# Loading two tokens to a partition in 512-byte rows for the first four units of a retention and FF kernel

## The chip, the cores and the metric

The kernel runs on one core of a Trainium2 chip. The metric is device time in microseconds (us) of one execution. Most executions of one kernel lie within about 1% of their mean here; each comparison with the kernel before was made on the same chip in the same rounds. The experiments ran in four sets with their own rounds and chips, so between sets the ratios say more than the medians. Every ratio is the mean time of one kernel's fast runs over the mean of the other's fast runs of the same rounds, so it is not quite the ratio of the medians that stand beside it.

## The reference, cut to what matters

```python
# q, k, v: (8 batches, 8 heads, 576 tokens, 64), fp32
scores = q @ k.T / 8
ret    = scores * Dmat                  # Dmat[i, j] = gamma_h ** (i - j) for i >= j, else 0
attn   = ret @ v
x      = attn, heads joined: (4608, 512)
out    = relu(x @ w_in) ** 2 @ w_out    # w_in (512, 2048), w_out (2048, 512)
```

The retention part is computed by chunks of 128 tokens ("units", 36 of them, 32 full and 4 made of tails of 64) with a state R that is carried from one chunk to the next. The FF part is most of the arithmetic.

## The kernel before: the parts that the change touches

Every instruction is a task in a small model of the machine inside the program. The model has durations and priorities (keys), and the order in which it starts the tasks is the order in which they are emitted. Each engine then has its own list in that order. An entry that waits can hold up those behind it: in run e11 below TensorE stands still for 2.53 us at one such entry, with FF work behind it.

```python
FIRST = ["u0", "u1", "u2", "u3", "w0", "w1", ..., "w7"]      # four units, then 8 weight blocks of 1 MB
WARM = 48                                                    # filler matmuls for the empty start

def add_load(u):                                             # on SyncE, three loads of 256 KB
    nc.sync.dma_start(out=x, in_=src[b, :, c*P:(c+1)*P, :].rearrange("h p d -> p h d"))   # rows of 64*4 = 256 B

def add_unit(u, base):
    # kq16 <- cast of k (GpSimd) and of q (ScalarE for the first four units, else GpSimd)
    # v16  <- v * vdec (GpSimd)
    # units 0..7: 8 transposes on TensorE into psT, then ScalarE (k) and VectorE (q) copy psT to kqT
    # units 8..:  one transposing DMA on SyncE writes kqT

# then, for each group of one or two units:
#   psc (scores), psS (chunk sums)      TensorE
#   rT = psc * mask, Rm, stmp, R        VectorE   (R is the state that the next unit reads)
#   psO (output)                        TensorE
#   xT = psO * gamma                    VectorE   -> the input of the FF
#   ph = xT @ w_in ; rl = relu ; gT = rl*rl ; po = gT @ w_out
# from group 3 on po is done by Strassen's scheme, which needs differences of weights, wT (VectorE)
```

Units 0 and 1 are groups of their own; units 2 and 3 are the third group, 4 and 5 the fourth. The SyncE queue holds loads, transposing DMAs and stores of the output in one list.

## Time and profile before

| | before |
|---|---|
| median, 6 runs (lowest to highest) | 303.44 us (302.53 to 305.68) |
| span of the profiled run | 301.3 us |
| TensorE busy | 286.8 us, 95% |
| DMA, 256 B rows / 2 KB rows | 219 / 383 GB/s |
| first FF matmul | 22.55 us |
| cast of the last weight block begins | 40.48 us |

How such a profile is read. An engine's busy share is an average over stages; what a stage is worth is read from what ended the wait there. A line of a timeline gives start and duration in us, engine, source line, operation, output<-inputs, and in brackets the idle time before it with what ended it. A line of the waits gives an engine's instruction, what released it, the total in us, the number of times and the longest. The prediction below shows the main lines of before. One thing it touches only in a figure is the hole at 134 us, so here is TensorE's timeline around its end, and the windows view of five microseconds of it (length, busy, count, granted clock, DMA share, GB/s):

```profile
133.38 0.60 PE L640 MATMUL ph<-xT,w_in 128*128 128x256 f16 x4
...
137.81 0.32 PE L307 MATMUL psc<-kqT 64*64 64x64 f16 x16 [3.46 <-DMA kqT<-kq]
138.06 1.47 PE L733 MATMUL po<-w_out,gS 128*128 128x256 f16 x8
139.33 1.92 PE L733 MATMUL po<-wT,gT 128*128 128x256 f16 x8
```

```profile
135.00:136.00 1.00, 0.00 (x0) 1.00 0.02 2
136.00:137.00 1.00, 0.00 (x0) 1.00 0.63 133
...
139.00:140.00 1.00, 1.00 (x7) 0.50 1.35 217
140.00:141.00 1.00, 1.00 (x6) 0.50 1.35 218
141.00:142.00 1.00, 1.00 (x6) 0.52 1.36 221
```

TensorE stands still for 3.46 us until a transposing DMA brings kqT, and then the granted clock is 0.50 for some 3.4 us. Half of 3.4 us is lost too, so the hole costs 3.46 + 1.7 = 5.2 us. From 135 to 136 us the DMA moved only 2 GB/s, so TensorE waits here for one chain and not for bytes in general: a q load issued at 127.86 us, its cast, and the transposing DMA issued at 132.90 (the 12th of the kernel, for unit 19). "Supply" below means such chains.

One profile shows one such slow stretch, which makes a mean clock of about 0.994 (an estimate: 1.7 of 301 us lost). Of the 104 runs of the kernel before in the experiments' rounds, 103 have a mean clock of 0.983 to 0.994, and 53 of them 0.989 or less. So nearly every run has at least one slow stretch, and about half seem to have a second, which the kept profile of before does not show.

### The profile page before, as it was taken

Reading aid. Unit: us, or ns where it says so; the run is one execution under the profiler, and the core shown is the slowest. Engines: PE = TensorE matmul, PEld = TensorE weight load, DVE = VectorE, ACT = ScalarE, POOL = GpSimd, SP = SyncE. Lnnn points to the kernel's source line nnn. Section 1 sums busy time; section 2 is a strip of 40 time slices with the busy share of each in tenths; the row PEclk is TensorE's granted clock in tenths of the full one; section 3 lists DMA queues with packets and bytes.
Section 4 is the critical chain, followed back from the end, with each engine's and each line's share of the span. In section 5 each row is a group of like instructions: output and inputs, shape, how many; then the busy total and the mean of one; then the engine's idle time right before and its main releaser. Section 6 shows DMA issues by size and latency. Waiting matters only on the chain.

```text
span 301.3 us, 10320 instructions
## 1 busy us (share of the span) xinstructions
PE 286.8 (95%) x4456; PEld 235.7 (78%) x4456; DVE 189.6 (63%) x409; ACT 186.6 (62%) x351; POOL 94.9 (31%) x125
## 2 busy tenths in 40 slices
PE   5988999999999999987999999999999999999995
PEld 2547865588888888865888888888888888888874
DVE  1476589777693949582876778567777676562410
ACT  4235972296757676741758575857585758558861
POOL 3433379434432332343242433243353200000000
PEclk9999999999999999997999999999999999999999
DMA  8999999889999997999999999999999520101012
GB/s 165 218 349 383 386 228 247 175 198 162 210 212 179 202 183 182 184 234 186 198 196 225 180 211 179 195 189 232 214 204 196 128 72 2 72 3 70 2 70 72
DMA packets 151742, 54.16 MB, mean 180 GB/s; under 512 B 142864, under 2 KB 143120, under 8 KB 151696
## 3 DMA queue, kind: packets, MB, share of 16 engines
q1 hardware_dynamic: 151248, 52.97, 90.2%
q8 instruction: 35, 0.57, 0.9%
q10 hardware_dynamic: 448, 0.52, 0.7%
q14 instruction: 11, 0.09, 0.1%
HBM read 36.70 MB, written 9.44 MB: 153 GB/s over the span
## 4 chain that ended last, share of the span: by engine, by line
PE 82%; DMA 6%; SPq 4%; DVE 3%; ACT 2%; issue 2%; POOL 1%
PE ph L640 41%; PE po L733 30%; PE psO L307 4%; SPq L263 4%; PE po L681 4%; DMA wi<-in_moe_w_in_dram 3%; DVE wT L597 2%; DMA kqT<-kq 2%; PE psc L307 2%; PE psS L307 2%; DMA q<-in_q_dram 1%; ACT rl L648 1%; ACT gT L658 1%; DVE xT L530 0%; POOL w_in L288 0%
## 5 line engine op out<-in xcount | busy, mean ns | idle before, releaser
L640 PE MATMUL ph<-xT,w_in 128*128 128x256 f16 (+1 forms) x1216 | 139.2, 268 | 1.7 <-POOL w_in L288 1.2
L640 PEld LDWEIGHTS <-w_in 128*128 128x128 f16 x1216 | 112.4, 98 | 15.5 <-POOL w_in L288 1.3
L648 ACT ACTIVATE rl<-ph 128x512 f16<-128x512 f32 x144 | 84.4, 588 | 49.8 <-PE ph L640 48.3
L658 ACT ACTIVATE gT<-rl 128x512 f16<-128x512 f16 x112 | 70.5, 630 | 3.5
L711 DVE TENSOR_TENSOR gS<-gT 128x512 f16<-128x512 f16 x60 | 29.9, 498 | 39.0 <-ACT gT L658 38.3
L333 POOL TENSOR_TENSOR v<-v,vdec_full 128x512 f16<-128x512 f32 x32 | 34.6, 1082 | 53.7 <-DMA v<-in_v_dram 49.6
L733 PEld LDWEIGHTS <-gS 128*128 128x128 f16 x480 | 46.0, 98 | 6.2 <-DVE gS L711 0.5
L733 PE MATMUL po<-wT,gS 128*128 128x256 f16 x360 | 49.0, 273 | 0.0
L733 PEld LDWEIGHTS <-gT 128*128 128x128 f16 x360 | 35.4, 99 | 4.5
L321 POOL CAST kq<-q 128x512 f16<-128x512 f32 x32 | 21.5, 673 | 39.1 <-DMA q<-in_q_dram 39.1
L321 POOL CAST kq<-k 128x512 f16<-128x512 f32 x36 | 23.7, 658 | 31.4 <-DMA k<-in_k_dram 28.3
L733 PE MATMUL po<-w_out,gT 128*128 128x256 f16 x240 | 31.1, 273 | 0.0
L530 DVE TENSOR_TENSOR xT<-psO,gam_full 128x512 f16<-128x512 f32 x36 | 23.9, 685 | 9.3 <-PE psO L307 9.0
L469 DVE TENSOR_TENSOR rT<-psc,mask 128x512 f16<-128x512 f32 x36 | 24.2, 685 | 8.7 <-PE psc L307 7.7
L660 DVE TENSOR_TENSOR gT<-rl 128x512 f16<-128x512 f16 x32 | 17.2, 549 | 12.3 <-ACT rl L648 12.1
L681 PE MATMUL po<-w_out,gT 128*128 128x512 f16 (+1 forms) x112 | 22.7, 349 | 0.3 <-ACT w_out L288 0.3
L756 DVE TENSOR_TENSOR o<-po,u 128x256 f32<-128x256 f32 x30 | 12.6, 419 | 11.0 <-ACT u L746 7.0
L227 PE MATMUL warm<-junk,ident 128*128 128x512 f16 x48 | 15.0, 451 | 3.0 <-DVE junk L205 3.0
L746 ACT COPY u<-po 128x256 f32<-128x256 f32 x30 | 11.0, 365 | 10.7 <-PE po L733 10.7
L498 DVE TENSOR_TENSOR R<-stmp,dec 128x256 f16<-128x256 f32 x32 | 16.4, 511 | 1.1
L681 PEld LDWEIGHTS <-gT 128*128 128x128 f16 x112 | 10.7, 98 | 8.0 <-issue 0.6
L776 ACT COPY o<-po 128x256 f32<-128x256 f32 x15 | 5.5, 367 | 18.2 <-PE po L733 18.1
(57 smaller groups left out, 253.0 us busy)
## 6 DMA issues: line engine op xcount, KB each, us to landing
k<-in_k_dram SPq DMA_DIRECT2D x32, 256.0 KB, 4.8
q<-in_q_dram SPq DMA_DIRECT2D x32, 256.0 KB, 4.7
v<-in_v_dram SPq DMA_DIRECT2D x32, 256.0 KB, 5.0
out_dram<-o SPq DMA_DIRECT2D x31, 256.0 KB, 3.2
wi<-in_moe_w_in_dram SPq DMA_DIRECT2D x4, 1024.0 KB, 10.4
wo<-in_moe_w_out_dram SPq DMA_DIRECT2D x4, 1024.0 KB, 9.2
k<-in_k_dram SPq DMA_DIRECT2D x8, 128.0 KB, 4.2
q<-in_q_dram SPq DMA_DIRECT2D x8, 128.0 KB, 4.7
```

Of the source, the lines that this page charges most:

```text
L307: nc.tensor.matmul(out_, lhsT=lhsT, rhs=rhs, start=start, stop=True, skip_group_check=True, tile_position=(64 * row, 64 * col))
L321: op(out=out_.rearrange("p (n b a d) -> p n b a d", n=2, b=2, a=2), in_=in_.rearrange("p (n a b) d -> p n b a d", n=2, a=2))
L333: nc.gpsimd.tensor_tensor(out=t, in0=tile_of["v32", u], in1=vdec[kind].rearrange("p (h o) -> p h o", o=1).to_broadcast([P, H, D]), op=ALU. ...
L469: nc.vector.tensor_tensor(out=r, in0=tile_of["psc", g][:, :, cols(s)].rearrange("p a (n i) -> p a n i", i=64), in1=mask.rearrange("p (o r ...
L530: nc.vector.tensor_tensor(out=tile_of["x", g][:, :, s * P:(s + 1) * P].rearrange("p n (c i) -> p c n i", c=2), in0=tile_of["psO", g][:, :, ...
L640: nc.tensor.matmul(tile_of["ph", g, fb][:, j, :], lhsT=w_in16[:, m, fi * P:(fi + 1) * P], rhs=tile_of["x", g][:, m, :], start=(m == 0), st ...
L648: nc.scalar.activation(out=t, in_=tile_of["ph", g, fb], func=ACTF.Relu)
L658: nc.scalar.activation(out=t, in_=rl, func=ACTF.Square)
L660: nc.vector.tensor_tensor(out=t, in0=rl, in1=rl, op=ALU.mult)
L681: nc.tensor.matmul(tile_of["po", u, lo], lhsT=tile_of["g", g][:, fi, s * P:(s + 1) * P], rhs=w_out16[:, fi, lo:hi], start=(fi == 0), stop= ...
L711: nc.vector.tensor_tensor(out=Sx(k, h), in0=in0(h), in1=in1(h), op=op)
L733: nc.tensor.matmul(tile_of["pb", g, bank], lhsT=left(i), rhs=right[:, i, :], start=(start and i == 0), stop=(i == HF - 1), skip_group_chec ...
```

## The change

Its intent: bring the first four units in faster, as their rows of 256 B move at 219 GB/s and the weights' at 383. Two neighbouring tokens of one head are contiguous in memory, so a partition that takes two tokens gets rows of 512 B. For k transposed and q transposed that layout does no harm (the copy from PSUM puts the tokens back in order), but k and v are also used with one token in a partition; matmuls with two 0/1 matrices bring them there. The pairs use the weights' buffers, the order of loads becomes pair, two weight blocks, pair, six blocks, and the R multiplications of these units go to GpSimd. Cut to its core:

```diff
+    perm = const.tile([P, 2, 2, P], FP16, name="perm")
+    nc.gpsimd.memset(perm, 0.0)
+    for s in range(2):
+        nc.gpsimd.affine_select(out=perm[:, s], ..., fill=1.0, base=-P * s, pattern=[[1, 2], [-1, P]], channel_multiplier=2)
-    WARM = 48
+    WARM = 40
+    PAIRED = 4
-    FIRST = ["u0", "u1", "u2", "u3", "w0", "w1", "w2", "w3", "w4", "w5", "w6", "w7"]
+    FIRST = ["p0", "w0", "w1", "p2", "w2", "w3", "w4", "w5", "w6", "w7"]
+    def add_load_pair(u):
+        for n, (name, src) in enumerate((("k", k), ("q", q), ("v", v))):
+            ... stage.tile([P, 2, H, 2 * D], FP32, name="pair", tag="wst")
+            nc.sync.dma_start(out=x, in_=src[b, :, c * P:(c + 2) * P, :].rearrange("h (p e) d -> p h (e d)", e=2))
+            loaded[...] = dma_task(0, 1.4 if loaded else 2.3, fn, ...)
+    def add_unit_pair(u, base):
+        # casts kx (GpSimd), qx (ScalarE), vx (GpSimd): 128x1024
+        # psT: 8 transposes each of kx and qx; copies to kqT reorder the tokens
+        for s in range(2):
+            for i, name in enumerate("kv"):
+                for e in range(2):
+                    nc.tensor.matmul(t, lhsT=perm[:, s, e, :], rhs=tile_of[name + "x", u][:, e, :], start=(e == 0), stop=(e == 1))
+                # k: ScalarE copies psn to kn;  v: VectorE multiplies psn by vdec into v16
-                nc.vector.tensor_tensor(          # R
+                (nc.gpsimd if u < PAIRED else nc.vector).tensor_tensor(
... (buffers are freed later accordingly)
```

More of the change, by code (lines that the diff above doesn't have):

```diff
@@ L161 @@
     make_identity(nc, ident)
+    perm = const.tile([P, 2, 2, P], FP16, name="perm")
+    nc.gpsimd.memset(perm, 0.0)
+    for s in range(2):
+        nc.gpsimd.affine_select(out=perm[:, s], in_=perm[:, s], compare_op=ALU.not_equal, fill=1.0, base=-P * s,
+                                pattern=[[1, 2], [-1, P]], channel_multiplier=2)
     iota_p = const.tile([P, 1], FP32, name="iota_p")
@@ L268, in add_load, with fn @@
             loaded[name, u] = dma_task(0, 1.2 if loaded else 2.1, fn, acq=("ld",) if n == 0 else ())
+    def add_load_pair(u):
+        b, c = units[u][1:]
+        for n, (name, src) in enumerate((("k", k), ("q", q), ("v", v))):
+            def fn(n=n, name=name, src=src):
+                if name != "q":
+                    tile_of["stage", u] = stage.tile([P, 2, H, 2 * D], FP32, name="pair", tag="wst")
+                x = tile_of[name + "32", u] = tile_of["stage", u][:, n % 2]
+                nc.sync.dma_start(out=x, in_=src[b, :, c * P:(c + 2) * P, :].rearrange("h (p e) d -> p h (e d)", e=2))
+            loaded[name, u] = loaded[name, u + 1] = dma_task(0, 1.4 if loaded else 2.3, fn,
+                                                             acq=("wst",) if name != "q" else ())
     def add_weight(i):
@@ L292, in add_weight @@
         wcast[i] = halves
-    ahead = 4
     for x in FIRST:
-        (add_load if x[0] == "u" else add_weight)(int(x[1:]))
+        (add_load_pair if x[0] == "p" else add_weight)(int(x[1:]))
     for u in range(NU):
@@ L315, in add_unit @@
         kind, b, c = units[u]
-        early = u < ahead
         tail = [tail_dec] if kind == "tail" else []
@@ L328, in fq @@
         def fq():
-            sorted_cast(nc.scalar.copy if early else nc.gpsimd.tensor_copy, tile_of["kq", u][:, 1], tile_of["q32", u])
+            sorted_cast(nc.gpsimd.tensor_copy, tile_of["kq", u][:, 1], tile_of["q32", u])
         def fv():
@@ L336, in add_unit @@
         ck = add("POOL", base, 0.65, fk, deps=[loaded["k", u]], acq=("kq",))
-        cq = add("ACT" if early else "POOL", base + 1, 0.62, fq, deps=[loaded["q", u], ck])
+        cq = add("POOL", base + 1, 0.62, fq, deps=[loaded["q", u], ck])
         cv = add("POOL", base + 2, 1.1, fv, deps=[loaded["v", u]] + tail, acq=("v16",))
@@ L367, in add_unit, with fc, ft, fe @@
             T["kqT", u].append(e)
+    def add_unit_pair(u, base):
+        xs = {}
+        for name, eng, op in (("k", "POOL", nc.gpsimd.tensor_copy), ("q", "ACT", nc.scalar.copy),
+                              ("v", "POOL", nc.gpsimd.tensor_copy)):
+            def fc(name=name, op=op):
+                t = tile_of[name + "x", u] = cast.tile([P, 2, H * D], FP16, name=name + "x", tag="kq16")
+                x = tile_of[name + "32", u].rearrange("p h (e d) -> p h e d", e=2)
+                if name == "v":
+                    op(out=t.rearrange("p e (h d) -> p e h d", d=D), in_=x.rearrange("p h e d -> p e h d"))
+                    return
+                for e in range(2):
+                    op(out=t[:, e].rearrange("p (n b a d) -> p n b a d", n=2, b=2, a=2),
+                       in_=x[:, :, e].rearrange("p (n a b) d -> p n b a d", n=2, a=2))
+            xs[name] = add(eng, base + "kqv".index(name), dict(k=1.3, q=1.2, v=1.2)[name], fc, deps=[loaded[name, u]],
+                           acq=("kq",))
+        sched.free("wst", [xs["k"], xs["q"]])
+        sched.free("wst", [xs["v"]])
+        T["kqT", u], T["kqT", u + 1] = [], []
+        readers = {"k": [], "q": [], "v": []}
+        for i, name in enumerate("kq"):
+            def ft(i=i, name=name):
+                t = tile_of["psT", u, i] = ps_ff.tile([P, 2, NP, P], FP16, name="psT", tag="ff")
+                for e in range(2):
+                    for x in range(NP):
+                        nc.tensor.transpose(t[:, e, x, :], tile_of[name + "x", u][:, e, x * P:(x + 1) * P], ident)
+            t = add("PE", base + L + 2 * i, 0.45, ft, deps=[xs[name]], acq=("ff",))
+            readers[name].append(t)
+            es = []
+            for s in range(2):
+                def fe(i=i, s=s):
+                    if i == 0:
+                        tile_of["kqT", u + s] = work.tile([P, 2 * NP, P], FP16, name="kqT", tag="kqT", bufs=6)
+                    (nc.vector.tensor_copy if i else nc.scalar.copy)(
+                        out=tile_of["kqT", u + s][:, i * NP:(i + 1) * NP].rearrange("p x (t e) -> p e x t", e=2),
+                        in_=tile_of["psT", u, i][:, :, :, half(s)])
+                es.append(add("DVE" if i else "ACT", base + L + 2 + 2 * s + i, 0.6, fe, deps=[t] + T["kqT", u + s] + es,
+                              acq=() if i else ("kqT",)))
+                T["kqT", u + s].append(es[-1])
+            sched.free("ff", es)
+        for s in range(2):
+            T["casts", u + s] = []
+            for i, name in enumerate("kv"):
+                def fp(s=s, name=name):
+                    t = tile_of["psn", u + s, name] = ps_ff.tile([P, H * D], FP32, name="psn", tag="ff")
+                    for e in range(2):
+                        nc.tensor.matmul(t, lhsT=perm[:, s, e, :], rhs=tile_of[name + "x", u][:, e, :], start=(e == 0),
+                                         stop=(e == 1))
+                def fn(s=s, name=name):
+                    ps = tile_of["psn", u + s, name]
+                    if name == "k":
+                        if s == 0:
+                            tile_of["kn", u] = cast.tile([P, 2, H * D], FP16, name="kn", tag="kq16")
+                        tile_of["kq", u + s] = tile_of["kn", u][:, s:s + 1]
+                        nc.scalar.copy(out=tile_of["kq", u + s][:, 0], in_=ps)
+                        return
+                    t = tile_of["v16", u + s] = cast.tile([P, H, D], FP16, name="v16", tag="v16")
+                    nc.vector.tensor_tensor(out=t, in0=ps.rearrange("p (h d) -> p h d", d=D),
+                                            in1=vdec["full"].rearrange("p (h o) -> p h o", o=1).to_broadcast([P, H, D]),
+                                            op=ALU.mult)
+                t = add("PE", base + L + 4 + 2 * s + i, 0.44, fp, deps=[xs[name]], acq=("ff",))
+                readers[name].append(t)
+                e = add("DVE" if i else "ACT", base + L + 6 + 2 * s + i, 0.7 if i else 0.6, fn, deps=[t],
+                        acq=("v16",) if i else (() if s else ("kq",)))
+                sched.free("ff", [e])
+                T["casts", u + s].append(e)
+        for name in "kqv":
+            sched.free("kq", readers[name])
@@ L505, in after_sums @@
             r1 = add("DVE", key + 0.2 + s, 0.42, fr1, deps=[r0])
-            r2 = add("DVE", key + 0.3 + s, 0.35, fr2, deps=[r1], acq=("R",))
+            r2 = add("POOL" if u < PAIRED else "DVE", key + 0.3 + s, 0.6 if u < PAIRED else 0.35, fr2, deps=[r1], acq=("R",))
             chain += [r0, r1, r2]
@@ L539, in add_casts @@
         for u in units_of(g):
+            if u < PAIRED:
+                if u % 2 == 0:
+                    add_unit_pair(u, base_of(group_of[u]) - L)
+                continue
             add_unit(u, base_of(g) - L * (2 if g > JOIN else 1) + 4 * (u - units_of(g)[0]))
@@ L553, in add_ret @@
             for u in units_of(g):
-                sched.free("kq", [t])
+                T["kqread", u] = t
             after_scores(g, t, base + 5)
@@ L573, in add_ret @@
             for u in units_of(g + 1):
-                sched.free("kq", [t2])
+                T["kqread", u] = t2
             after_outs(g, t1, t2, base + 30.4)
@@ L794 @@
     for u in range(NU):
+        if u >= PAIRED:
+            sched.free("kq", [T["kqread", u]])
+        elif u % 2:
+            sched.free("kq", [T["kqread", u - 1], T["kqread", u]])
+    for u in range(NU):
         if ("Rread", u) in T:
```

## The prediction

> **What bounds the kernel now.** I read the page first (busy shares and the 40 slices), then the chain of waits, the DMA view of two windows, the waits of TensorE, and last the timelines of single engines. The page's slices of 7.5 us, with PE, DMA share, and the rate moved:
>
> ```profile
> span 301.3 us, 10320 instructions
> PE   5988999999999999987999999999999999999995
> DMA  8999999889999997999999999999999520101012
> GB/s 165 218 349 383 386 228 247 175 198 162 210 212 179 202 183 182 184 234 186 198 196 225 180 211 179 195 189 232 214 204 196 128 72 2 72 3 70 2 70 72
> ```
>
> TensorE is busy 95% of the span, so work is the bound in most of it. But 48 of its matmuls (15.0 us busy) are warm-up fillers, and nearly all lie before 22 us: there it has little to do. The rates say why: 218 GB/s in the second slice, where the first four units of q, k and v come in, and 383 to 386 GB/s in the fourth and fifth, where the weights do. The DMA view of 4 to 14 us and of 22 to 32 us puts sizes to it:
>
> ```profile
> DMA packets 8682, 2.19 MB, mean 219 GB/s; under 512 B 8682, under 2 KB 8682, under 8 KB 8682
> ...
> DMA packets 1909, 3.83 MB, mean 383 GB/s; under 512 B 54, under 2 KB 54, under 8 KB 1906
> ```
>
> All packets of the first window are under 512 B (one token of one head, 64 x 4 = 256 B); those of the second are 2 KB. The chain of waits shows the start as one line of load issues, each about 1.15 us, then the first weight block, its cast, and the first FF matmul:
>
> ```profile
> 11.22 1.15 SPq L263
> 12.42 1.14 SPq L263
> 13.60 7.80 DMA wi<-in_moe_w_in_dram
> 21.46 1.05 POOL w_in L288
> 22.55 1.98 PE ph L640 x32
> ```
>
> The weights follow at 2.7 us a block; the last one lands at 40.4, as GpSimd's timeline shows, with the casts of unit 4 behind it, and the x of units 4 and 5 reaches TensorE at 58.46:
>
> ```profile
> 40.48 1.04 POOL L288 CAST w_out<-wo 128x1024 f16<-128x1024 f32 x1 [1.79 <-DMA wo<-in_moe_w_out_dram]
> 41.48 0.79 POOL L321 CAST kq<-k 128x512 f16<-128x512 f32 x1
> ...
> 58.46 0.61 PE L640 MATMUL ph<-xT,w_in 128*128 128x256 f16 x4 [0.48 <-DVE xT L530]
> ```
>
> At 58.46 TensorE had waited only 0.48 us. So both things must move if the rest is to move: the work on the first four units, and the supply of units 4 and 5. After 60 us TensorE is full but for one hole:
>
> ```profile
> PE psc L307 <- DMA kqT<-kq: 3.5, 1, 3.5
> PE psO L307 <- issue: 1.3, 1, 1.3
> PE ph L640 <- POOL w_in L288: 1.2, 1, 1.2
> ```
>
> The first of these lies at 134.35 to 137.81. It traces back to a q load and a transposing DMA behind it, so supply is close to the edge up to there.
>
> **What the Trainium skill says.** (1) "DMA: Bandwidth & Descriptors", Specifications: at least 512 B a transfer for line rate, with a read-modify-write below. The trace agrees that 256 B is slow (219 against 383 GB/s); nothing in it is 512 B. (2) The same page, "Why small descriptors are slow (HBM only)": each packet has a fixed overhead, so larger ones gain without a step. The two rates fit that as well as they fit (1), and this is the main uncertainty below. (3) "SBUF — State Buffer", "Who interferes with whom": GpSimd and VectorE exclude each other on a shared port pair. The trace agrees: a kq cast takes 0.61 us alone and 1.0 to 1.1 us between 46 and 51 us, while VectorE runs the wT differences. (4) "TensorE: Matmul & The Clock Gate", "HAM oscillation": idle gaps over about 3.4 us drop the clock. After the gap of 3.46 us eight 256-column matmuls took 1.92 us, where they take 1.04 elsewhere, so such a hole costs about 4.5 us, not 3.5.
>
> **The change, part by part.**
>
> *Removed: 256 B rows in the first four units.* They move 4 x 3 x 262,144 B = 3.146 MB. At 218 GB/s that is 14.4 us. In 512 B rows: a 2 KB packet takes 2048 / (383/16) = 85.6 ns on one of 16 engines, a 256 B packet 256 / (219/16) = 18.7 ns. A line through both has a slope of 0.0373 ns a byte and a fixed part of 9.1 ns, so 512 B take 28.2 ns: 290 GB/s, or 10.8 us, 3.6 us saved. If 512 B already reach the weights' 383 GB/s, it is 8.2 us, 6.2 us saved. I choose between them, nearer to the middle: about 335 GB/s, 9.4 us, **5.0 us saved**. Issuing won't eat it: six issues replace twelve, with as many rows each (1,024), and the very first issue took 0.45 us where nothing was queued.
>
> *Moved: the order.* Now two units, two weight blocks, two units, six blocks. The first block should land near 0.8 + 2.1 (first issue to data) + 4.7 (1.57 MB) + 2.7 = 10.3 us instead of 21.4, and the first FF matmul start near 11.5 instead of 22.55. This gives TensorE about 4 us of FF work (two units by two blocks, 64 matmuls of 128 columns, 1.98 us per 32) before block 2 is in. But the last block can't come sooner than its bytes allow: 40.4 - 5.0 = 35.4 us. FF work on four units is 27.3 us by the durations in the program, and it needs all of the weights, so TensorE gets ahead in this stretch and then meets units 4 and 5, whose loads are queued behind the last block. Those move by the DMA saving alone. So **the eleven us at the first matmul are not the gain; the 5 us at the last block are.**
>
> *Added on TensorE:* 16 permuting matmuls of 512 columns, 16 x 0.22 = 3.5 us (the po matmul of 512 columns runs at 0.216 a piece). They fall before about 20 us, where fillers ran; 8 fillers (some 2.5 us) go. Off the path.
>
> *Added on ScalarE:* 4 copies of k, PSUM to SBUF, 128x512: 4 x 0.59 = 2.4 us. *On VectorE:* 4 scalings of v, 4 x 0.69 = 2.8 us, less the 4 R multiplications (4 x 0.42 = 1.7 us at their usual length) that go to GpSimd. *On GpSimd:* the 4 multiplications of v (4 x 1.04) become two plain casts of 128x1024 (2 x 1.04); with R's four at about 0.6 that is -4.2 + 2.1 + 2.4 = +0.3 us. The permutation constant adds a memset and two selects, about 1.3 us from the 0.29 of the identity's, but the first cast waited 1.89 us for data. The windows view of 12 to 21 us has VectorE busy 6.74 of 9 us (75%), ScalarE 2.89 and GpSimd 3.02, so there is room. The latency from loaded v to scores grows by about a matmul and an eviction, 1.2 us a pair. That delays x of units 2 and 3, expected near 25 us, when TensorE still has blocks 2 and 3 for units 0 and 1.
>
> *After 36 us:* the casts of unit 4 start 5.0 us earlier; VectorE has less leftover squaring when wT begins, which I put at 0.5 us in the run to 58.46. Sum: **-5.5 us**, and I expect it to pass through, as TensorE has no idle reserve between 60 and 280 us.
>
> **Rivals.** *A: the rate is a step.* At 383 GB/s the gain is 6.2 + 0.5, about 6.7 us, 297.1 us. For it: the page's 512 B. Against it: the straight-line fit. *B: the line holds.* Then it is 3.6 + 0.5, about 4 us, 299.7 us. *C: the latency of the permuted path becomes the bound,* x of units 2 and 3 late, with TensorE idle between 15 and 25 us. For it: each pair now has 8 evictions, split over two engines that also do weight casts and relu. Against it: the idle shares above, and the slack of 8 us that the earlier weight blocks make; it would make 301 to 303 us. *D: the hole at 134 us changes.* The order of instructions comes from durations in a model in the program, which this change feeds differently. The hole can close (4.5 us more gain, about 294 us), or another appear (about 302 us). The trace speaks for neither: GpSimd waits 48 us for loads between 60 and 140 us, so supply is tight with or without the change. *E: the load is hidden anyway.* The chain through the load issues speaks against it.
>
> **Range and chances.** Before is 303.79 us; 303.79 - 5.5 = 298.3 us. A and B span 297.1 to 299.7; D widens both ends, C the upper: 294.5 to 301.8. The border of 2% is 297.7 us, just under my centre; A and a closed hole lie beyond it: 0.41 faster, 0.55 within, 0.04 slower.
>
> **What would show it.** In the first 17 us a rate of 290 to 383 GB/s; first FF matmul near 11.5 us; last weight cast on GpSimd starting near 35.5 us; the first FF matmul of units 4 and 5 near 53 us, with a longer wait than 0.48 us; the 134 us hole near 129 us; end near 296 us of span. The prediction is wrong if that wait for units 4 and 5 eats the 5 us, if the rate stays under 270, or if holes differ after 60 us.

## The result, and the profile after

The changed kernel takes 300.40 us (median of 6, 299.15 to 301.63) against 303.44 us for the kernel before in the same rounds; all runs are fast ones. The ratio is 0.9892 with a 95% interval of 0.9851 to 0.9934: 1.1% faster, within 2%. The predicted 298.3 us was 2.1 us too low; the measured time is inside its range. All six runs of the changed kernel have a mean granted clock of 1.00.

Lines of the changed kernel have other numbers: the FF products ph are L730 (before L640), po L771 and L823 (L681, L733), xT L616 (L530), the weight casts L306 (L288). The page's span and slices:

```profile
span 298.7 us, 10350 instructions
PE   4997999999999999999899999999999999999995
DMA  8999989999899999999899999989999820201012
GB/s 198 360 334 385 338 192 245 174 197 178 201 207 210 214 149 191 177 185 178 198 192 229 187 179 220 193 203 195 220 186 229 143 72 2 72 3 72 0 72 70
```

The second slice moves 360 GB/s instead of 218, but it holds weights too. The DMA view of 14 to 17.5 us, in which only pairs are moved, gives the rate of 512 B rows:

```profile
DMA packets 2018, 1.02 MB, mean 291 GB/s; under 512 B 32, under 2 KB 2018, under 8 KB 2018
```

The timelines of TensorE, VectorE and GpSimd at the start (the first is the last permuting group of pair 2; the second is the first FF work; then x of unit 0, of units 2 and 3, of units 4 and 5; then the last weight block's cast):

```profile
21.34 1.04 PE L432 MATMUL psn<-vx,perm 128*128 128x512 f16 x4
22.22 0.89 PE L730 MATMUL ph<-xT,w_in 128*128 128x128 f16 x13
...
17.65 0.69 DVE L616 TENSOR_TENSOR xT<-psO,gam_full 128x512 f16<-128x512 f32 x1 [0.88 <-PE psO L324]
...
33.09 1.29 DVE L616 TENSOR_TENSOR xT<-psO,gam_full 128x512 f16<-128x512 f32 x2 [0.86 <-PE psO L324]
...
55.67 1.29 DVE L616 TENSOR_TENSOR xT<-psO,gam_full 128x512 f16<-128x512 f32 x2 [0.34 <-PE psO L324]
...
37.41 1.27 POOL L306 CAST w_out<-wo 128x1024 f16<-128x1024 f32 x1 [1.79 <-DMA wo<-in_moe_w_out_dram]
```

The last weight block comes 3.07 us sooner (37.41 against 40.48). But x of unit 0 comes later (17.65 against 14.60 in before), x of units 2 and 3 six us later (33.09 against 27.10), and the FF work starts at the same time as before, 22.22 us. And TensorE's waits:

```profile
PE ph L730 <- issue: 1.6, 2, 1.0
PE psc L324 <- DMA kqT<-kq: 1.3, 1, 1.3
```

The wait for transposing DMAs, 3.5 us before, is down to 1.3, at 145.65 us, and the clock stays at 1.00 behind it. It is not the same wait made shorter. The 12th transposing DMA, for which the kernel before waits, is issued at 129.44 us instead of 132.90, and nothing waits for it now. The wait that is left is for the 14th, one group later: it is issued at 143.80 us, against 143.70 in before, so there supply comes no sooner.

Where the time went is best seen in the moments at which x of a unit is finished, as x is the hand-over from retention to FF. They are the ends of the xT instructions in VectorE's timeline (us, one profile each):

| x of unit | 0 | 3 | 5 | 11 | 15 | 17 | last | span |
|---|---|---|---|---|---|---|---|---|
| before | 15.29 | 28.39 | 58.41 | 92.73 | 122.90 | 145.54 | 268.84 | 301.3 |
| after | 18.34 | 34.38 | 56.96 | 93.77 | 123.56 | 142.05 | 266.33 | 298.7 |
| after - before | +3.1 | +6.0 | -1.5 | +1.0 | +0.7 | -3.5 | -2.5 | -2.6 |

(The count of x is in order of time; a pair of units in one line of the timeline ends at the end of the line.) This is not the picture that was predicted. At unit 15 the changed kernel is *behind*, by 0.7 us. All of its gain appears between units 15 and 17, which is the hole at 134 us.

Why earlier weights freed nothing is seen in before itself. The windows view of the stretch in which the last blocks land (length, busy, count, granted clock, DMA share, GB/s) has TensorE busy all the time:

```profile
27.00:41.00 14.00, 14.00 (x172) 1.00 1.05 352
```

After its first FF matmul the waits view of before lists one wait for weights, of 0.3 us, which ends at 42.83. TensorE was bound by its own work, so an earlier last block alone could not help it.

### The profile page after: what moved, and what is told of

It is laid out like the page before. It is cut to its first block, busy times and chain, and to the rows that moved or that the text cites. A ratio compares the mean times of both kernels' runs of the same rounds, so it can differ in the third digit from the quotient of the medians.

```text
span 298.7 us, 10350 instructions
## 1 busy us (share of the span) xinstructions
PE 285.4 (96%) x4464; PEld 235.4 (79%) x4464; DVE 194.1 (65%) x409; ACT 189.5 (63%) x355; POOL 97.8 (33%) x130
## 4 chain that ended last, share of the span: by engine, by line
PE 72%; DMA 10%; DVE 7%; ACT 4%; SPq 3%; issue 2%; POOL 1%; DVEq 0%
PE ph L730 35%; PE po L823 27%; DMA wi<-in_moe_w_in_dram 7%; PE po L771 4%; PE psO L324 4%; DMA q<-in_q_dram 3%; ACT rl L738 2%; ACT gT L748 1%; DVE wT L687 1%; DVE gT L750 1%; PE psS L324 1%; PE psc L324 1%; DVE gS L801 1%; SPq L270 1%; DMA kqT<-kq 1%
## 5 line engine op out<-in xcount | busy, mean ns | idle before, releaser
L730 PE MATMUL ph<-xT,w_in 128*128 128x256 f16 (+1 forms) x1216 | 139.5, 267 | 2.2 <-issue 1.6
L730 PEld LDWEIGHTS <-w_in 128*128 128x128 f16 x1216 | 112.6, 98 | 16.7 <-issue 1.9
L801 DVE TENSOR_TENSOR gS<-gT 128x512 f16<-128x512 f16 x60 | 30.5, 510 | 40.8 <-ACT gT L748 40.0
L823 PEld LDWEIGHTS <-gS 128*128 128x128 f16 x480 | 46.0, 98 | 5.7
L823 PE MATMUL po<-wT,gS 128*128 128x256 f16 x360 | 49.0, 273 | 0.0
L349 POOL TENSOR_TENSOR v<-v,vdec_full 128x512 f16<-128x512 f32 x28 | 30.4, 1086 | 34.2 <-DMA v<-in_v_dram 31.1
L823 PEld LDWEIGHTS <-gT 128*128 128x128 f16 x360 | 35.0, 98 | 4.5 <-issue 0.3
L337 POOL CAST kq<-k 128x512 f16<-128x512 f32 x32 | 22.0, 688 | 42.4 <-DMA k<-in_k_dram 41.7
L337 POOL CAST kq<-q 128x512 f16<-128x512 f32 x32 | 22.2, 693 | 33.4 <-DMA q<-in_q_dram 33.2
L823 PE MATMUL po<-w_out,gT 128*128 128x256 f16 x240 | 31.1, 273 | 0.0
L616 DVE TENSOR_TENSOR xT<-psO,gam_full 128x512 f16<-128x512 f32 x36 | 23.9, 685 | 8.6 <-PE psO L324 8.5
L750 DVE TENSOR_TENSOR gT<-rl 128x512 f16<-128x512 f16 x32 | 18.0, 569 | 10.4 <-ACT rl L738 10.2
L771 PE MATMUL po<-w_out,gT 128*128 128x512 f16 (+1 forms) x112 | 23.2, 349 | 0.0
L846 DVE TENSOR_TENSOR o<-po,u 128x256 f32<-128x256 f32 x30 | 12.6, 420 | 9.3 <-ACT u L836 6.3
L801 DVE TENSOR_TENSOR gS<-gT,gS 128x512 f16<-128x512 f16 x30 | 16.7, 557 | 1.0
L801 DVE TENSOR_TENSOR gS<-gS,gT 128x512 f16<-128x512 f16 x30 | 15.6, 520 | 1.0
L771 PEld LDWEIGHTS <-gT 128*128 128x128 f16 x112 | 10.5, 98 | 7.0
L823 PE MATMUL po<-wT,gT 128*128 128x256 f16 x120 | 15.6, 273 | 0.4 <-DVE o L846 0.4
```

What stands on the lines that cost most here:

```text
L337: op(out=out_.rearrange("p (n b a d) -> p n b a d", n=2, b=2, a=2), in_=in_.rearrange("p (n a b) d -> p n b a d", n=2, a=2))
L349: nc.gpsimd.tensor_tensor(out=t, in0=tile_of["v32", u], in1=vdec[kind].rearrange("p (h o) -> p h o", o=1).to_broadcast([P, H, D]), op=ALU. ...
L616: nc.vector.tensor_tensor(out=tile_of["x", g][:, :, s * P:(s + 1) * P].rearrange("p n (c i) -> p c n i", c=2), in0=tile_of["psO", g][:, :, ...
L730: nc.tensor.matmul(tile_of["ph", g, fb][:, j, :], lhsT=w_in16[:, m, fi * P:(fi + 1) * P], rhs=tile_of["x", g][:, m, :], start=(m == 0), st ...
L750: nc.vector.tensor_tensor(out=t, in0=rl, in1=rl, op=ALU.mult)
L771: nc.tensor.matmul(tile_of["po", u, lo], lhsT=tile_of["g", g][:, fi, s * P:(s + 1) * P], rhs=w_out16[:, fi, lo:hi], start=(fi == 0), stop= ...
```

## The experiments

All experiments were timed in three rounds beside the kernel before. Ratios are to the kernel before. "Theory S" says that the change's gain reaches the end only as supply: loads of later units are 3 us earlier at the hole. "Theory P" is the prediction's: the whole program moves forward.

**e1 and e2: supply made plentiful, in both kernels.** The loads of full units from unit 4 on take contiguous rows of 2 KB. The bytes and the order of instructions are the same; the result is wrong on purpose.

```diff
-  in_=src[b, :, c * P:(c + 1) * P, :].rearrange("h p d -> p h d")
+  in_=src[b].rearrange("h s d -> (h s) d")[1024 * c:1024 * (c + 1)].rearrange("(p e) d -> p (e d)", e=8)   # u >= 4
```

> The kernel before, with the loads of all full units from unit 4 on taken as contiguous rows of 2 KB (the same bytes, a wrong result on purpose; the order of instructions is unchanged). Supply behind the weights is then no limit. Theory S (the change's gain reaches the end only because units behind the weights arrive earlier at the hole at 134 us; TensorE itself is no further ahead before it): the hole of 3.5 us and the slow clock after it vanish, so about 4.5 us faster than before, near 299 us. Theory P (earlier weights move the whole program forward, as predicted): the same here; the pair with e2 tells them apart.

> The changed kernel with the same wide loads from unit 4 on (a wrong result on purpose). Theory S: not faster than e1; from the x of units 14 to 17, 0.7 us later than before in the two profiles, I expect 0 to 2 us slower than e1. Theory P: faster than e1 by the 3 us by which the last weight block comes earlier.

| | median | ratio (95%) | x of 5 | x of 15 | x of 17 | span |
|---|---|---|---|---|---|---|
| e1, kernel before + plenty | 300.01 | 0.9897 (0.9843 to 0.9950) | 58.04 | 122.85 | 140.33 | 297.2 |
| e2, changed kernel + plenty | 300.98 | 0.9922 (0.9883 to 0.9960) | 56.77 | 124.14 | 141.46 | 298.4 |

The windows view of e1 over the stretch of the old hole (length; PE, PEld, DVE, ACT, POOL busy; clock; DMA share; GB/s) has TensorE busy throughout at full clock:

```profile
130.00:150.00 20.00, 20.00 (x405) 17.23 (x404) 16.73 (x34) 12.89 (x25) 8.90 (x12) 1.00 1.00 220
```

In e1 the 12th transposing DMA is issued at 128.27 us, 4.6 us earlier than in before. With supply out of the way the change gains nothing: e2 is not faster than e1 (the medians differ by 1.0 us the other way; the intervals overlap, so "slower" is not shown). The profiles say why: up to unit 15 e1 is where before is (122.85 against 122.90), so before's TensorE was not held by supply until then; at unit 17 it is 5.2 us ahead, just the cost of the hole worked out above. The changed kernel gains 0.3 us of span from plenty, and nothing by the ratios (0.9922 against 0.9892). So theory S holds here, and theory P, which expected e2 3 us ahead of e1, falls.

Two numbers now stand beside each other for each kernel: what TensorE's own path allows (the span with plenty) and what came out. Before: 297.2 and 301.3, so supply set the end. After: 298.4 and 298.7, so both set it nearly together, and more supply alone would give the changed kernel little. These are spans of single profiles, and runs of one kernel differ by 1 to 2 us: e1's profile is its fastest run, and by the ratio e1 gains about 3.1 us, not 4.1.

**e3: the row size alone undone.** The same tiles, order and engines, but two loads of 256 B rows in place of each pair load.

```diff
-  nc.sync.dma_start(out=x, in_=src[...].rearrange("h (p e) d -> p h (e d)", e=2))
+  for e in range(2):
+      nc.sync.dma_start(out=x.rearrange("p h (e d) -> p h e d", e=2)[:, :, e],
+                        in_=src[...].rearrange("h (p e) d -> p h e d", e=2)[:, :, e])
```

> The changed kernel with only the row size undone: each pair load becomes two of 256 B rows into the same tile, order on all other engines unchanged. DMA time of the four units goes from 10.8 back to 14.4 us. Theory S: last weight cast 3.6 us later, x from unit 10 up to 120 us moves by less than 2 us, and the hole near 140 us grows from 1.3 to about 4.5 us; the end 3 to 4 us later, 303 to 305 us. Theory P: all x from unit 4 on move by 3.6 us and the hole stays at 1.3 us, with about the same end.

Measured: 304.61 us, ratio 1.0052 (1.0026 to 1.0078), so slower than the changed kernel (by 4.2 us in the medians of different rounds, by 4.9 us from the two ratios), and 0.5% slower than the kernel before. The rows are worth somewhat more than the 3.6 us of DMA time that they save, and the rest of the change costs 1 to 1.6 us. (The edit also doubles the number of these loads; that was not tested apart.) The last weight cast begins at 41.81, 4.4 us later than in the changed kernel. But the path by which this reaches the end was not the expected one: x of unit 5 comes 4.5 us later (61.42) and stays 5 us later up to unit 15 (128.58), and there is no wait for a transposing DMA at all. Within the paired kernel a later start does pass through TensorE's path; it arrives so late at 140 us that supply no longer limits. My line for theory S ("x moves by less than 2 us, the hole grows") was wrong, theory P's (all x 3.6 us later) came nearer, and the picture of two paths, of which the later one counts, explains both: here TensorE's path is the later one.

**e4: R back on VectorE.** In the changed kernel's timeline GpSimd makes R of unit 3 at 30.17, behind a weight cast, though its input was ready at 29.39.

```diff
-  (nc.gpsimd if u < PAIRED else nc.vector).tensor_tensor(
+  nc.vector.tensor_tensor(          # and the task goes to "DVE", 0.35
```

> The changed kernel with the first four R multiplications back on VectorE. In the profile of the changed kernel R of unit 3 waits on GpSimd behind a weight cast and is ready 1.6 us after its input, and a pair's cast of k waits behind R on GpSimd. Theory: x of units 2 and 3 comes 1 to 3 us earlier than 33.1 us. Under S the end moves by less than 1.5 us, as the supply at 140 us is unchanged; under P it moves by as much as x of units 4 and 5 does.

Measured: 300.90 us, ratio 0.9906 (0.9874 to 0.9938), the same as the changed kernel. x of unit 3 came at 34.63 (34.38 in the changed kernel), not 1 to 3 us earlier. Moving R is not seen to be the cost.

**e5, e6, e7: the order of the first loads.** e5 puts both pairs ahead of the weights in the changed kernel, e6 does that with plenty of supply, and e7 gives the kernel before the mixed order.

```diff
-  FIRST = ["p0", "w0", "w1", "p2", "w2", ...]      # e5, e6
+  FIRST = ["p0", "p2", "w0", "w1", "w2", ...]
-  FIRST = ["u0", "u1", "u2", "u3", "w0", "w1", "w2", ...]      # e7
+  FIRST = ["u0", "u1", "w0", "w1", "u2", "u3", "w2", ...]
```

> The changed kernel with only the order of the first loads undone: both pairs first, then the eight weight blocks (the last block keeps its time, as the bytes before it are the same). Theory O (the order costs TensorE's path what the rows gain: x of units 2 and 3 at 34 us instead of 28 because the second pair waits behind two weight blocks): x of units 2 and 3 near 28 us or earlier, and x up to unit 15 some 2 to 4 us earlier than in the changed kernel. Then the supply sets the end, as before, and the hole near 140 us is back at 2 to 4 us: the end within 1 us of the changed kernel's. Theory L (the latency of the paired path is the cost): x of units 2 and 3 still later than 30 us, x up to unit 15 unmoved.

> The same order with the wide rows from unit 4 on (a wrong result on purpose), so that supply sets no limit. Theory O: 2 to 4 us faster than e2 (298.4 us of span), near 295. Theory L: the same as e2 within 1 us.

> The kernel before with only the order changed as in the change: two units, two weight blocks, two units, six blocks. Theory O: x of units 2 and 3 some 5 us later (33 us), x up to unit 15 later by 2 to 5 us, and the hole at 134 us gone, as TensorE comes late to it; the end within 1.5 us of before. Theory L: x from unit 4 on within 1 us of before and the hole as before.

| | median | ratio (95%) | x of 3 | x of 5 | x of 15 | span |
|---|---|---|---|---|---|---|
| e5 | 300.99 | 0.9899 (0.9824 to 0.9975) | 33.66 | 57.48 | 125.37 | 299.7 |
| e6 | 301.33 | 0.9928 (0.9907 to 0.9948) | 30.99 | 57.71 | 125.45 | 299.4 |
| e7 | 304.53 | 0.9996 (0.9959 to 1.0032) | 33.61 | 59.62 | 124.13 | 299.9 |

In the paired kernel the mixed order is not the cost: with both pairs first, x up to unit 15 comes 1.8 us later, not earlier, and e6 is not faster than e2. The hole of 2 to 4 us that e5 was to bring back did not come: TensorE has no wait for a transposing DMA there. In the kernel before, the mixed order does delay x of unit 3 by 5.2 us and x of unit 15 by 1.2 us, shortens the wait for transposing DMAs from 3.5 to 1.3 us (in two pieces), and leaves the time where it was. The profiled run of e7 was its fastest (its fast runs went from 301.81 to 305.16 us, one slow run took 306.68), so its span says less than its ratio. e5 and e6 have the same instructions up to 28 us and differ by 2.7 us in x of unit 3: single profiles of this stretch vary by that much.

**e8: stores on ScalarE, on top of e5.**

```diff
-  eng = nc.scalar if group_of[u] == len(groups) - 1 else nc.sync
+  eng = nc.scalar          # and the store tasks go to "ACT"
```

> A try for a faster kernel: the order of e5, and all stores of the output issued by ScalarE instead of SyncE, so that loads do not stand in one queue behind stores that wait for their data. If the hole near 140 us is a load that waited behind a store, it goes, and the end is near e6's, 296 us; if it is the rate of the loads, the end is that of e5[...].

Measured: 313.08 us, ratio 1.0325 (1.0242 to 1.0407). The waits of TensorE show the price: 2.4 us and 2.2 us for relu on ScalarE and 2.4 us for VectorE's sums, which were at most 0.3 us in e5. A store that waits for its data on ScalarE holds up the relu behind it: in the timeline ScalarE stands idle from 97.0 to 100.65 us, issues a store and then runs the next square and relu, and TensorE waits until 102.20. It does not answer whether loads behind stores made the hole.

**e9, e10: the start fitted to measured times.** The constant for the permutations is built last on GpSimd, the filler's input first on VectorE, and the program's model gets the durations that the profile shows.

```diff
-  WARM = 40, fillers of 0.3; pair loads 1.4 if loaded else 2.3
+  WARM = 28, fillers of 0.43; pair loads 1.8 if loaded else 2.7
+  # perm is built after the masks; memset(junk) comes first on VectorE
```

> The changed kernel with its start made to fit the measured times: the constant for the permutations built last on GpSimd and the filler's input first on VectorE (the fillers started at 4.4 us), 28 fillers of 0.43 us in the program's model of the schedule (measured 0.43 us, the model had 40 of 0.3), and pair loads of 1.8 us there (measured 1.7 to 1.8, the model had 1.4). Theory L (TensorE's path is late because the first pairs' x is late: 18.3 us for unit 0, 34.4 us for unit 3, first FF matmul at 22.2): x of unit 0 near 15.5 us, first FF matmul before 20 us, x of unit 3 some 2 us earlier, x up to unit 15 1 to 3 us earlier. The end gains less, as supply then limits again at 140 us: 0 to 1.5 us against the changed kernel. The rival, theory W (work on TensorE and VectorE between 35 and 58 us sets the path, whatever x does): x of unit 4 and later within 0.7 us of the changed kernel.

> e9 with the wide rows from unit 4 on (a wrong result on purpose). Theory L: 1 to 3 us faster than e2 (298.4 us of span). Theory W: within 0.7 us of e2.

| | median | ratio (95%) | x of 0 | x of 3 | x of 5 | x of 15 | span |
|---|---|---|---|---|---|---|---|
| e9 | 300.04 | 0.9875 (0.9807 to 0.9944) | 15.84 | 32.60 | 55.34 | 122.45 | 298.0 |
| e10 | 300.95 | 0.9928 (0.9900 to 0.9956) | 15.88 | 32.66 | 55.20 | 123.79 | 298.0 |

x of unit 0 came 2.5 us earlier, x of unit 3 1.8 us, x of unit 5 1.6 us, x of unit 15 1.1 us: as theory L (late x of the first pairs makes TensorE's path late) has it. The first FF matmul came at 20.96, not before 20. The end is not separable from the changed kernel's (0.9875 against 0.9892, with overlapping intervals), and neither is e10 from e2, where 1 to 3 us had been expected.

**e11: units 8 and 9 transposed by TensorE, on top of e9.**

```diff
-  XBAR = 8
+  XBAR = 10
```

> A try for a faster version: e9, with units 8 and 9 transposed by TensorE and not by the DMA, which takes two transposing DMAs out of the supply ahead of the hole at 140 us and puts 16 matmuls and 4 evictions (about 1 us of TensorE) on the engines. If e9's TensorE path is ahead and supply sets its end, this is 0 to 1 us faster than e9; if TensorE's own path sets it, about 1 us slower.

Measured: 302.91 us, ratio 0.9984 (0.9957 to 1.0011), slower than e9 by 2.9 us in the medians of the same rounds; at most about 1 us had been expected. x of unit 5 is as in e9 (55.04), x of unit 11 is 7.7 us later (100.41): the first transposes of unit 8 or 9 sit in TensorE's list ahead of FF work and wait 2.5 us in one piece, at 69.5 us, for VectorE's copy of kqT, and the granted clock behind it is 0.61 and then 0.50 up to 75 us.

**e12: FF work of units 0 and 1 ahead of the second pair, on top of e9.**

```diff
-  base = us[0] * L
+  base = us[0] * L - (400 if g < 2 else 0)     # keys of the first product of groups 0 and 1
```

> e9 with one change more: in the program's schedule the first FF products of units 0 and 1 go ahead of the second pair's transposes and permutations. Theory F (TensorE's path did not move in the change because its FF work began no earlier, 22.2 us against 22.55, so that 3 us more of it was left when the last weight block landed 3 us sooner): first FF matmul near 16 us instead of e9's 21.0, x of units 4 to 15 some 1 to 2 us earlier than in e9, and a longer wait for supply near 140 us, so the end within 1 us of e9's. If x of units 4 to 15 does not come earlier although the FF work starts 5 us sooner, theory F is not the whole cause, and what bounds TensorE's path between 35 and 58 us stays open.

Measured: 302.06 us, ratio 0.9920 (0.9883 to 0.9957). The first FF matmul came at 15.34, 5.6 us before e9's. x of unit 5 came 0.3 us earlier than in e9, and yet x of units 7 to 15 came 2.5 us *later*. The second pair had to wait, x of unit 3 came at 37.59, and TensorE ran empty at 33.5 to 35.2 us. Theory F in that form falls. But the run shows what does count, and it can be counted in all kernels.

**What is left when the last weight block is there.** From then on TensorE has everything for the first four units and is nearly always busy up to 130 us, so its path is that moment plus the FF work still left. The FF work of the first four units is 128 ph of 128 columns, 64 ph of 256 and 64 po of 512. The groups view, from 0 to the start of the last weight cast, counts what is done. Before (to 40.48 us):

```profile
L640 PE MATMUL ph<-xT,w_in 128*128 128x128 f16 x128 | 7.8, 219 | 1.2 <-POOL w_in L288 1.2
L640 PE MATMUL ph<-xT,w_in 128*128 128x256 f16 x59 | 7.3, 273 | 0.0
L681 PE MATMUL po<-w_out,gT 128*128 128x512 f16 x8 | 2.1, 379 | 0.0
```

After (to 37.41 us):

```profile
L730 PE MATMUL ph<-xT,w_in 128*128 128x128 f16 x128 | 8.3, 219 | 2.2 <-issue 1.6 <-POOL w_in L306 0.6
L771 PE MATMUL po<-w_out,gT 128*128 128x512 f16 x9 | 2.6, 381 | 0.0
L730 PE MATMUL ph<-xT,w_in 128*128 128x256 f16 x16 | 2.0, 272 | 0.0
```

Before, 5 ph of 256 columns and 56 po are left. The chain of waits has 40 such ph in 4.37 us (0.109 each) and 10 po in 2.16 us (0.216 each), so 5 x 0.109 + 56 x 0.216 = 12.6 us are left. After, 48 and 55 are left: 17.1 us. The block came 3.1 us sooner, but 4.5 us more work waited for it: the path moves by +1.4 us. Of the 4.5 us, 3.1 are no loss: an always busy TensorE has that much less done at a moment 3.1 us earlier. The other 1.4 us are work that it is behind. The same count for the other kernels, each from its own profile (e8 and e11 are left out, as they have other holes before unit 15):

| | last cast | ph 256 done | po done | left, us | path against before | x of 15 against before |
|---|---|---|---|---|---|---|
| before | 40.48 | 59 | 8 | 12.6 | 0 | 0 |
| after | 37.41 | 16 | 9 | 17.1 | +1.4 | +0.7 |
| e1 | 40.29 | 64 | 9 | 11.9 | -1.0 | -0.1 |
| e2 | 37.06 | 16 | 10 | 16.9 | +0.8 | +1.2 |
| e3 | 41.81 | 25 | 12 | 15.5 | +4.2 | +5.7 |
| e4 | 37.06 | 12 | 8 | 17.8 | +1.7 | +1.1 |
| e5 | 37.25 | 0 | 8 | 19.2 | +3.4 | +2.5 |
| e6 | 37.13 | 10 | 12 | 17.1 | +1.1 | +2.6 |
| e7 | 41.20 | 44 | 11 | 13.6 | +1.7 | +1.2 |
| e9 | 37.34 | 27 | 12 | 15.3 | -0.5 | -0.5 |
| e10 | 36.95 | 24 | 12 | 15.6 | -0.6 | +0.9 |
| e12 | 37.06 | 0 | 11 | 18.4 | +2.4 | +2.1 |

(In e5 three of the 128-column ph are missing as well.) The count follows the measured shift within about 1.5 us in every row, with single profiles on both sides and the possibility of a missing record. It is a balance of work and not an experiment: it says how far TensorE is behind, not why. The differing column is the ph of 256 columns: the first FF product of units 2 and 3, which can't start before their x. That is 34.38 us in the changed kernel and 28.39 before. But x is not all that holds them: in e6 it came at 30.99, and only 10 were done, as TensorE was still at the 128-column ph of units 0 and 1 until about 36 us.

**What stays open.** Why the second pair's x is 6 us late is only partly accounted for. Its v is cast from 19.57 us, against 17.51 for unit 3's v before: 2.1 us of it. The other 3.9 us lie on the path from v to x, and e4, e5 and e9 take away single parts of that (R on GpSimd: nothing; the order: 0.7 us; the late start: 1.8 us) and not the whole. As single profiles of this stretch can differ by 2.7 us, none of these parts is shown by itself. The profile puts 1.6 us of TensorE's waits there to "issue", which names no cause. And no run shows whether a kernel with an earlier x of units 2 and 3 and with more supply at 140 us would be faster; no version that beats the changed kernel was found, e9 being no better than equal.

## Why the prediction was right or wrong

The range held and the likeliest outcome came, "within 2%". The reason given for it was half wrong, and that the number came near was partly luck: the forecast gain of 5.5 us at the start did not pass through, and a hole that the forecast left out of its sum closed and gave 3.0 us instead.

- **What bounds the start, right.** The loads of 256 B rows were on the way to the first weights, and faster rows brought the last block sooner. e3 shows the rows worth 4 to 5 us within the paired kernel. But the last block was not what held TensorE, which was busy from 27 to 41 us of before.
- **The rate, mis-sized.** The working had a straight line through 256 B and 2 KB that gave 290 GB/s at 512 B; the profile has 291. I then chose "nearer to the middle: about 335 GB/s ... 5.0 us saved", leaning on the Trainium skill's statement about 512 B ("DMA: Bandwidth & Descriptors", Specifications). The term measured 3.07 us at the last block. Rival B's rate was the right one, rival A's step isn't there.
- **The step that failed: "TensorE gets ahead in this stretch".** It rested on a first FF matmul near 11.5 us and on x of units 2 and 3 "near 25 us". They came at 22.22 and 33.1 to 34.4 us. The weights were not late: the cast of the first block began at 11.44 us. The FF needs x as well, and x of unit 0 came at 15.29 us even in before, so 11.5 could not be reached; here it came at 18.34. Then the second pair's transposes and permutations, which I had called off the path, stood in TensorE's list until 22.22 (e12, with the FF ahead of them, began it at 15.34). I had costed the added casts, matmuls and evictions as work (they do fit beside the rest) and allowed 1.2 us a pair for them as a delay. So TensorE began its FF work when it had before, and by the count above it was 1.4 us behind at the last block instead of ahead. This is rival C, which I had put at 301 to 303 us; it happened on TensorE's path and did not make the end that late, because the hole closed.
- **"I expect it to pass through", wrong.** The first FF matmul of units 4 and 5, forecast near 53 us, started at 59.50, against 58.46 in before, and up to unit 15 nothing had come through (+0.7 us). With supply plentiful in both kernels (e1, e2) the change gains nothing.
- **The hole, named as rival D but not put to use.** I had about the right size for it (4.5 us guessed; 5.2 us at unit 17 and 4.1 us of span in e1) and its cause, supply. But I treated it as a lottery of the schedule, and added it on top of the 5.5 us. It is where the gain came from: the transposing DMA for which the kernel before waits is issued 3.5 us sooner, TensorE comes 0.7 us later, so that wait and the slow clock behind it are gone, and a wait of 1.29 us for a later transposing DMA is left. 298.7 us of span is then near what TensorE's path allows (298.4 in e2).
- **Costs off the path, right in part.** VectorE's, ScalarE's and GpSimd's added work was not seen to be the end by itself (only the R part was tested, in e4). But putting the wT differences "5.0 + 0.5 us" earlier for units 4 and 5 was wrong in what it meant: their x came 1.5 us earlier, but TensorE still had 14 po of the first units to do from 55.73 us on, so an earlier x there bought nothing.

## What to carry to other kernels

Before you expect an earlier transfer to pay, count the work left on the bound engine at the moment it lands; if that grows by as much as the transfer came sooner, nothing moves. Look first whether the engine waits in that stretch at all. Where two paths (an engine's work and its supply) meet at a late point, make one plentiful in a run: what is then left is set by the other, and a change that speeds up only the one gains at most the difference. And a layout that is cheaper to load but needs more steps before its first use has to be judged by the latency to that use, not by the busy time that it adds.

## What the Trainium skill lacked or had wrong

- "DMA: Bandwidth & Descriptors", Specifications, gives 512 B as the smallest transfer for line rate. Here 512 B rows loaded at 291 GB/s and 2 KB rows at 383: three quarters. The prediction's straight line through 256 B and 2 KB gave 290 GB/s ahead of the run. The page's fixed overhead per packet, in "Why small descriptors are slow (HBM only)", is the better guide.
- The same page, "Where 436 GB/s comes from", has about 358 GB/s bind for transfers between HBM and SBUF. One core alone loaded weights at 377 to 394 GB/s in every 2 us from 22 to 34 us of the changed kernel; the page's own note on single-core figures fits that better.
- "TensorE: Matmul & The Clock Gate", "HAM oscillation", warns of idle gaps over about 3.4 us. The gap of 3.46 us did bring a clock of 0.50 for some 3.4 us. But shorter gaps did it too: after a wait of 1.66 us in e12, with small matmuls behind it, the clock was 0.50 from 36 to 39 us, and after one of 2.53 us in e11 it was 0.50 from 73 to 75 us. A wait of 2.37 us in e8 (until 102.20 us) and the one of 1.29 us in the changed kernel left it at 1.00. So the length of the gap alone does not decide here; no run shows what else does.
- No page says that the latency of a load's whole path to its first use should be counted when its layout changes; here x of units 2 and 3 came 6.0 us later, 3.9 us of it after the cast of v, although the last weight block came 3.07 us sooner.
